# Output gates by tanh per chunk, one decay buffer refilled by halves, and a first chunk written out by hand

## The chip, the cores and the metric

The kernel runs on 1 core of one Trainium2 chip. The metric is device time in microseconds, from the start of the program to its end. Three timed runs of the kernel before gave 734.65 (median), 732.61 and 736.13; the execution that was profiled took 732.55, of which the profile's span is 730.6.

## The reference

Three stages follow each other. The first is a gated linear attention with a matrix state for every batch and head (4 batches, 8 heads, 768 tokens, 40 channels):

```python
m_new  = maximum(f_gate[t] + m, i_gate[t])
f_stab = exp(f_gate[t] + m - m_new);  i_stab = exp(i_gate[t] - m_new)
C = f_stab * C + i_stab * outer(v[t], k[t]);  n = f_stab * n + i_stab * k[t]
y[t] = sigmoid(o_gate[t]) * (C @ q[t]) / maximum(abs(n @ q[t]), 1)
```

The second is a mixture of 8 experts with one expert per token (320 to 1024 to 320), the third a gated layer of width 1536 with a sigmoid gate. Only the first stage is touched by the change.

## The kernel before, in words

The attention is computed in 24 chunks of 128 tokens (`NTILE`), 6 chunks (`NC`) to a batch. For a chunk, TensorE makes the matrix of log decays of all pairs of tokens (`dec`, L626), ScalarE takes its exponential (`exp`), TensorE makes the scores of q and k (`sc`), VectorE multiplies the two (`pf`), TensorE multiplies by v (`out_`, L665) on top of the part that comes from the state (`inter`), and POOL and TensorE build the update of the state (`kw`, `state`; then `Cm`, `C`, `cb`). Two groups of four heads each are worked on one after the other (`dec0`, `dec1`). After it come the denominator (`abs`, `den`), the output gate over the denominator (`sod`, POOL), the product (`x`), its split into two half-precision parts (`xh`, `xla`, `xl`), transposes and their evacuation by ScalarE (`tr`, `ev`), and the router's logits (`log`, `lg`).

All engines are scheduled by hand. `ORDER` (L40) lists the parts of one step with the lag in chunks: `sod:2` in step n works on chunk n-2. `step(n)` (L911) runs through that list once, and each engine executes in the order in which instructions are written. The entries `r:1` and `r:2` pull pieces from a generator, `step.route`: routing work of a group of chunks, or, in the first steps, the pieces of `rest()` (L597) and `second()` (L614).

The log decays come from gate sums. `gates(x)` (L481) makes them for all batches, one half (3 chunks of each batch) at a time, as a chain on VectorE with one piece on POOL and casts on ScalarE. `store(x)` writes them to DRAM, and `decay` (L411) reads them back into rows 0 to 15 of two operand tiles, `at` and `rt`, whose other rows hold a fixed pattern (`pattern_at`, `pattern_rt`). There are two pairs of these tiles: the first is for batches 0 and 2, the second for 1 and 3. The first pair is filled by halves, and from batch 1 on a whole batch is loaded in one go when the batch's first chunk is loaded. Chunk 0 does not wait for this way through DRAM: its `dec` (L628) adds up 16 small matmuls for each group of heads out of the gate rows themselves.

The raw output gates of a batch are one DMA of 960 KB on POOL's queue (`output_gates`, L448), written in steps 0 to 2 for batches 1 to 3. Batch 0's are turned into sigmoids by one ScalarE instruction in step 0 (L957), the other three batches' by three instructions at the start of step 5 (L923). Each time an exponential of a small tile is written behind (L958, L924). The loads of q, k (`load_qk`, three buffers) and v (`load_v`) are issued by SP in the order written; a load waits at its issue for the buffer to come free, and all later loads of SP wait behind it.

`begin()` (L551) writes the start: memsets by POOL, loads by SP and ScalarE, the first half of the gate chain, `store(0)`, `decay`. `warm(n)` (L590) writes n matmuls of zeros that keep TensorE active and whose result nobody reads: 26 in `begin`, and 4, 4, 8 and 6 in step 0. `to_end(x)` (L531) transposes the factors of a half to tokens on partitions: transposes, a VectorE copy, a small product on VectorE, a matmul, a copy.

Of the kernel before, what the change touches and what calls it, by code (L numbers as in the profile page):

```python
# [41 lines left out]
    Cm:0 r:1 log:3 scat:0 xh:2 r:1 out0:1 pf1:0 r:1 out1:1 lg:3 xla:2 inter:0 state:0 r:1 xl:2 abs:1 den:1  # L42
# [17 lines left out]
def fused(ctx, tc, a, out, dbg=None):  # L60
# [312 lines left out]
    with ExitStack() as att:  # L373
# [11 lines left out]
        ats = [a1.tile([KM, 2, 2, S], F16, name=f"at{i}") for i in range(2)]  # L385
        rts = [a1.tile([KM, 2, NC, NP, T], F16, name=f"rt{i}") for i in range(2)]
# [24 lines left out]
        def decay(b, c0=0, c1=NC):  # L411

            at, rt = ats[b % 2], rts[b % 2]
            tk = slice(c0 * T, c1 * T)
            src = a_d[:, :, 2 * b:2 * b + 2, tk].rearrange("n h g s -> (n h) g s")
            if c1 - c0 == NC:
                SP_.dma_start(out=at[0:8].rearrange("p i g s -> p i (g s)"),
                              in_=src.rearrange("p g s -> p (g s)").unsqueeze(1).to_broadcast([8, 2, 2 * S]))
            else:
                for i in range(2):  # L420
                    SP_.dma_start(out=at[0:8, i, :, tk], in_=src)
            for g in range(2):
                SP_.dma_start(out=rt[8:16, g, c0:c1].rearrange("p c h t -> p (c h t)"),
                              in_=L_d[:, 2 * b + g, :NP * LR].rearrange("n (h x) -> n h x", h=NP)[:, :, c0 * NP * T:c1 * NP * T])

        def load_qk(m):
            m.at, m.rt = ats[m.b % 2], rts[m.b % 2]
# [17 lines left out]
        def gate(b):  # L445
            return sos[b * NC // HT][:, b * NC % HT:][:, :NC]

        def output_gates(b, queue):  # L448

            queue.dma_start(out=gate(b).rearrange("p c h d -> p c (h d)"), in_=a["o"][b])  # L450
# [21 lines left out]
        def pattern_at(i, cs, copy):  # L472
            for k in range(2):
                copy(ats[i][:, k].rearrange("p g (c t) -> p g c t", t=T)[:, :, cs],
                     cat[:, k:k + 1, :].unsqueeze(1).to_broadcast([KM, 2, len(range(NC)[cs]), T]))

        def pattern_rt(i, cs):
            V.tensor_copy(rts[i][:, :, cs].rearrange("p g c h t -> p g c (h t)"),
                          crt.rearrange("p h t -> p (h t)").unsqueeze(1).unsqueeze(1).to_broadcast([KM, 2, len(range(NC)[cs]), NP * T]))
# [71 lines left out]
        def begin():  # L551

            G.memset(kws[1], 0.0)
            G.memset(blank, 0.0)
            A.activation(blank, blank, AF.Exp)
            warm(26)
            G.memset(qks[0], 0.0)
# [6 lines left out]
            SP_.dma_start(out=con[:, 0:2 + NP], in_=a["cc"])  # L564
            SP_.dma_start(out=own_row, in_=a["own_row"])
            load_qk(chunks[0])
            load_v(chunks[0])
            blocks_empty()
            SP_.dma_start(out=c32, in_=a["c32"])
            pattern_at(0, H0, lambda o, i: A.activation(o, i, AF.Copy))  # L570
            for t, name in ((c16, "c16"), (tok, "tok"), (wgl_s, "wgl"), (ctab, "ctab")):
                A.dma_start(out=t, in_=a[name])
# [7 lines left out]
            G.memset(Cbs[1], 0.0)  # L580
            pattern_rt(0, H0)
# [3 lines left out]
            decay(0, 0, HC)  # L585
            exps(0)
            load_qk(chunks[2])
            load_v(chunks[2])

# [7 lines left out]
        def rest():  # L597

            yield from gates(1)
# [8 lines left out]
            yield True  # L608
            yield True
            exps(1)  # L610
            decay(0, HC, NC)
            yield True

        def second():  # L614

            pattern_at(1, H0, V.tensor_copy)
            yield True
            pattern_rt(1, H0)
            yield True
            pattern_at(1, H1, V.tensor_copy)  # L620
            yield True
            pattern_rt(1, H1)
            yield True


        def dec(m, g):  # L626
# [12 lines left out]
            for i, rows in ((0, KM), (1, KM - 1)):  # L639
                cols = slice(64 * i, 64 * i + 64)  # L640
                PE.matmul(m.pw[g][:, :, cols], m.at[:rows, i, g, m.tk], m.rt[:rows, g, m.c, :, cols], start=True, stop=True)
# [83 lines left out]
        def sod(m):  # L725
            m.sod = ap_.tile([128, H, D], F32, name="sod")
            G.tensor_tensor(m.sod, sos[m.t // HT][:, m.t % HT], m.den.unsqueeze(2).to_broadcast([128, H, D]), ALU.mult)

        def x(m):
# [5 lines left out]
            V.scalar_tensor_tensor(m.x.rearrange("p (h d) -> p h d", d=D), m.po[:, :, 0:D], SX, m.sod, ALU.mult, ALU.mult)  # L735
# [111 lines left out]
        parts = dict(kw=kw, gs=gs, inter=inter, state=state, Cm=Cm, C=C, cb=cb, abs=abs_, den=den, sod=sod,  # L847
# [63 lines left out]
        def step(n):  # L911
# [3 lines left out]
            for i in LOADS.get(n, ()):  # L915
                load_weights(i)
            if 1 < n < NTILE - 2:
                load(chunks[n + 2])
            if n == 3:
                step.route = second()  # L920
            if n == 5:
                for b in range(1, B):
                    A.activation(gate(b), gate(b), AF.Sigmoid)  # L923
                A.activation(blank, blank, AF.Exp)  # L924
            for name, lag in order:
# [6 lines left out]
                elif name in ("tr", "ev", "log", "lg") and n >= NTILE or name == "kw" and n == 0:  # L932
                    pass
                elif 0 <= n - lag < NTILE:
# [9 lines left out]
                    if n == 0 and name == "exp0":  # L944
                        step.route = rest()
                    if n == 0 and name in ("sc0", "sc1"):
                        warm(4)
                    if n == 0 and name == "pf0":
                        to_end(0)
                        warm(8)  # L950
                        kw(chunks[0])
                    if n == 0 and name == "state":
                        warm(6)
# [61 lines left out]
        UPS = 6  # L1015
# [3 lines left out]
        with tc.manual_schedule(engines=manual):  # L1019
            begin()  # L1020
            step.drain = False
            for n in range(NTILE + 2):
# [397 lines left out]
```

## Time and profile before

| | |
|---|---|
| timed runs | 734.65 us median (732.61 to 736.13) |
| profiled execution | 732.55 us, span 730.6 us |
| TensorE busy | 704.7 us, 96% |
| VectorE, ScalarE, POOL busy | 400.6, 327.8, 116.9 us |
| mean granted TensorE clock | 0.981 |
| attention stage | about 0 to 152 us |
| ACT_TABLE_LOAD | 6, of 1.28 us each: L555, L957, L958, L923, L924, L1164 |

PE is TensorE's matmuls, PEld its weight loads, DVE VectorE, ACT ScalarE, SP the engine that issues most DMAs; a `q` behind the name (SPq, ACTq) is that engine's instruction queue with DMA issues and waits. A granted clock of 1.00 is 2.4 GHz and 0.50 is 1.2 GHz. Times of a timeline are counted from the span's start.

### The profile page before, as it was taken

How to read it: one execution, taken by the hardware profiler on the slowest of the kernel's cores; microseconds unless marked ns; L12 is line 12 of the kernel's file. 1: busy time of each engine (PE TensorE's matmuls, PEld its weight loads, DVE VectorE, ACT ScalarE, POOL GpSimd, SP SyncE). 2: the span in 40 equal slices, each digit the busy share in tenths (PEclk: the TensorE clock that was granted, in tenths of full speed). 3: DMA queues.
4: the chain of work that ended last, by engine and by line, in shares of the span. 5: the costliest groups of instructions: out<-in, count | busy, mean ns of one | idle time of the engine just before them, and what ended most of it. 6: DMA issues, size and time to landing. Idle time of an engine off the chain costs nothing. (4 is left out here: it accounts for less than half of the span.)

```text
span 730.6 us, 15424 instructions
## 1 busy us (share of the span) xinstructions
PE 704.7 (96%) x6069; PEld 495.0 (68%) x6069; DVE 400.6 (55%) x920; ACT 327.8 (45%) x763; POOL 116.9 (16%) x152
## 2 busy tenths in 40 slices
PE   8879999979989999999999999999999999999998
PEld 5668999967656675766755676666666666666665
DVE  5756878747778888888786830322303223132130
ACT  4687777726465666555554511322313223132231
POOL 4433466733111111111100000000000000000000
PEclk8998999999999999999999999999999999999999
DMA  6573455643999897984414203001020010000000
GB/s 192 182 222 105 145 183 182 216 136 103 267 272 274 259 288 224 261 231 140 133 57 109 55 19 89 3 9 46 1 55 1 10 46 1 28 1 10 19 1 27
DMA packets 66407, 84.02 MB, mean 115 GB/s; under 512 B 41253, under 2 KB 48630, under 8 KB 66334
## 3 DMA queue, kind: packets, MB, share of 16 engines
q1 hardware_dynamic: 62844, 70.62, 34.5%
q0 software_dynamic: 3056, 12.28, 4.7%
q8 instruction: 48, 0.79, 0.5%
q14 instruction: 25, 0.20, 0.1%
q10 hardware_dynamic: 434, 0.14, 0.1%
HBM read 57.53 MB, written 17.16 MB: 102 GB/s over the span
## 5 line engine op out<-in xcount | busy, mean ns | idle before, releaser
L125 PE MATMUL pa<-xT,wgv 128*128 128x384 f16 x1536 | 252.6, 327 | 2.1 <-DVE hh L1170 2.1
L125 PEld LDWEIGHTS <-wgv 128*128 128x128 f16 x1536 | 150.8, 98 | 102.4 <-issue 4.3
L1165 DVE SCALAR_TENSOR_TENSOR gt<-pa,sg 128x384 f32<-128x384 f32 x96 | 53.5, 557 | 225.0 <-PE pa L125 193.1
L1183 PE MATMUL pb<-wo,hh 128*128 128x320 f16 x864 | 118.5, 299 | 0.0
L1164 ACT ACTIVATE sg<-pa 128x384 f32<-128x384 f32 x96 | 47.0, 489 | 142.6 <-PE pa L125 142.5
L1183 PEld LDWEIGHTS <-hh 128*128 128x128 f16 x864 | 84.5, 98 | 33.2
L358 PE MATMUL pb<-w,hh 128*128 128x320 f16 (+4 forms) x624 | 87.3, 299 | 0.2
L125 PE MATMUL pa<-xT,w 128*128 128x384 f16 (+5 forms) x576 | 82.5, 304 | 2.6 <-DVE hh L348 2.6
L125 PEld LDWEIGHTS <-w 128*128 128x128 f16 x640 | 56.2, 99 | 34.3 <-issue 4.6
L358 PEld LDWEIGHTS <-hh 128*128 128x128 f16 (+4 forms) x624 | 62.7, 101 | 23.6 <-DVE hh L348 1.2
L112 DVE SCALAR_TENSOR_TENSOR w<-ws,w 128x512 f16<-128x512 f32 (+1 forms) x92 | 56.1, 639 | 6.2 <-ACT w L111 6.0
L111 ACT ACTIVATE w<-ws 128x512 f16<-128x512 f32 (+1 forms) x92 | 50.4, 592 | 15.0 <-DMA ws<-in_w 14.9
L1185 ACT ACTIVATE ob<-pb 128x320 f32<-128x320 f32 x24 | 10.5, 437 | 100.5 <-PE pb L1183 100.5
L650 PE MATMUL ps<-qk 128*128 128x128 f32 x384 | 51.9, 279 | 1.5 <-DMA qk<-in_qk 1.5
L1170 DVE TENSOR_TENSOR hh<-gt,hh 128x384 f16<-128x384 f32 x96 | 52.6, 548 | 0.7
L1169 ACT ACTIVATE hh<-gt 128x384 f16<-128x384 f32 x96 | 49.5, 516 | 6.0 <-DVE gt L1165 5.9
L650 PEld LDWEIGHTS ps<-qk 128*128 128x128 f32 x384 | 47.7, 195 | 2.7 <-issue 1.9
L369 POOL DMA_INDIRECT y_d<-yr,own x24 | 26.4, 1098 | 131.3 <-DVE w L112 40.0
L655 DVE TENSOR_TENSOR pf<-ps,w 128x512 f32<-128x512 f32 x48 | 32.9, 685 | 20.6 <-ACT w L645 18.0
L347 ACT ACTIVATE hh<-pa 128x384 f16<-128x384 f32 (+6 forms) x80 | 33.7, 432 | 14.9 <-PE pa L125 14.6
L348 DVE SCALAR_TENSOR_TENSOR hh<-pa,hh 128x384 f16<-128x384 f32 (+6 forms) x80 | 36.1, 477 | 5.0 <-ACT hh L347 4.8
L645 ACT ACTIVATE w<-pw 128x512 f32<-128x512 f32 x48 | 28.5, 593 | 6.6 <-PE pw L637 3.6
(192 smaller groups left out, 700.0 us busy)
## 6 DMA issues: line engine op xcount, KB each, us to landing
ws<-in_w SPq DMA_DIRECT2D x24, 512.0 KB
vk<-in_vk SPq DMA_DIRECT2D x24, 324.0 KB
qk<-in_qk SPq DMA_DIRECT2D x48, 160.0 KB
ws<-in_w SPq DMA_DIRECT2D x15, 480.0 KB
ws<-in_wg SPq DMA_DIRECT2D x9, 512.0 KB
ws<-in_wv SPq DMA_DIRECT2D x9, 512.0 KB
hh<-in_o POOLq DMA_DIRECT2D x4, 960.0 KB, 7.8
ws<-in_wo SPq DMA_DIRECT2D x8, 480.0 KB
```

The lines of the kernel that those rows point to most:

```text
L111: A.activation(hi, src, AF.Copy, scale=scale)
L112: low = lambda: V.scalar_tensor_tensor(lo, src, scale, hi, ALU.mult, ALU.subtract)
L125: PE.matmul(ps, r if swap else l, l if swap else r, start=n == 0, stop=n == len(steps) - 1)
L347: A.activation(self.hh[:, 0, f], ph, AF.Relu)
L348: V.scalar_tensor_tensor(self.hh[:, 1, f], ph, 0.0, self.hh[:, 0, f], ALU.max, ALU.subtract)
L358: PE.matmul(py, self.hh[:, x, k, sl], w2[:, y, k, :], start=k == 0 and x + y == 0, stop=k == K1 - 1 and x == 1)
L650: PE.matmul(m.ps[g][:, p, :], m.k2[:, g, p], m.q2[:, p], start=True, stop=True)
L1164: A.activation(sg, pgv[0], AF.Sigmoid, scale=1.0 / (SY * SWG))
L1165: V.scalar_tensor_tensor(gt, pgv[1], SGT / (SY * SWV), sg, ALU.mult, ALU.mult)
L1169: A.activation(self.gh[:, 0, f, :], box[0], AF.Copy)
L1170: V.tensor_sub(self.gh[:, 1, f, :], box[0], self.gh[:, 0, f, :])
L1183: PE.matmul(po, self.gh[:, x, k, sl], wo[:, y, k * DM:(k + 1) * DM], start=k == 0 and x + y == 0, stop=k == K2 - 1 and x == 1)
```

## The change

The sigmoid is written as (tanh(o/2) + 1)/2. Two new parts, `th` (ScalarE) and `th1` (POOL), do this in place for each chunk, one lag after the chunk; the factor 1/2 goes into the scale of `x`. The bulk Sigmoids of steps 0 and 5 are gone. The gates are loaded by half batches, the first two by POOL at the start and the other six by SP in every third step.

There is one pair `at`, `rt`. `decay(u)` refills one half of it (three chunks); it is written in every third step. `pattern_at` for both halves is made by ScalarE in `begin`, `pattern_rt` by VectorE, the second half in `rest`; `second()` is gone.

The start has another order: the pattern's source is loaded by ScalarE's queue, memsets move ahead of the gate chain or behind it (a copy of 8 elements of `L` by POOL holds back what follows it), one q/k buffer and the state's two operand tiles are zeroed by ScalarE. Step 0 is replaced by `first()`, which writes the parts of chunk 0 in their own order, its outputs included, with fewer filler matmuls and with two pieces of the second half of the gate chain ahead. The load of chunk 3 moves from the end of step 1 to `rest`, behind `decay(1)`.

```diff
 ORDER = """
-    Cm:0 ... inter:0 state:0 r:1 xl:2 abs:1 den:1
+    Cm:0 ... inter:0 state:0 r:1 xl:2 abs:1 th:1 den:1 th1:1
...
-        def decay(b, c0=0, c1=NC):
-            at, rt = ats[b % 2], rts[b % 2]
+        def decay(u):
+            b, c0 = u // 2, u % 2 * HC
+            c1 = c0 + HC
...
-            if m.first and m.b:
-                decay(m.b)
             load_qk(m)
             load_v(m)
...
+        def output_gates(u, queue):
+            c0 = u % 2 * HC
+            queue.dma_start(out=gate(u * HC, HC)..., in_=a["o"][u // 2][:, c0:c0 + HC])
...
         def begin():
+            copy = lambda o, i: A.activation(o, i, AF.Copy)
+            A.dma_start(out=con[:, 0:2 + NP], in_=a["cc"])
+            A.dma_start(out=own_row, in_=a["own_row"])
             G.memset(kws[1], 0.0)
             G.memset(blank, 0.0)
             A.activation(blank, blank, AF.Exp)
-            warm(26)
-            G.memset(qks[0], 0.0)
+            warm(WARM)
             V.memset(mm[:, 0:1], -1e30)
             G.memset(keep, 1.0)
             G.memset(c3(keep)[:, :, 0:1], 0.0)
-            G.memset(qks[1], 0.0)
+            G.memset(qks[0], 0.0)
+            G.memset(kws[0], 0.0)
...
+            copy(qks[1].rearrange("q x p t -> q x (p t)"), zeros.unsqueeze(1).to_broadcast([128, 3, NP * T]))
+            pattern_at(H0, copy)
+            pattern_at(H1, copy)
             for _ in gates(0):
                 pass
-            G.memset(kws[0], 0.0)
+            G.tensor_copy(blank, L[0:1, S // 2 - 8:S // 2])
             output_gates(0, G)
-            for t in (Cbs[0], qks[2]):
-                G.memset(t, 0.0)
+            G.memset(qks[2], 0.0)
+            output_gates(1, G)
+            pattern_rt(H0)
             factors(0, V)
...
+        def first():
+            m = chunks[0]
+            dec(m, 0)
+            dec(m, 1)
+            later = gates(1)
+            for _ in range(2):
+                next(later)
+            for g in range(2):
+                exp(m, g)
+                sc(m, g)
+                pf(m, g)
+            warm(2)
+            for t in Cbs:
+                A.activation(t.rearrange("q p j d -> q (p j d)"), kws[1]..., AF.Copy)
+            to_end(0)
+            kw(m)
+            for g in range(2):
+                out_(m, g)
+            state(m)
+            warm(3)
+            for t, name in ((c16, "c16"), (tok, "tok"), (wgl_s, "wgl"), (ctab, "ctab")):
+                A.dma_start(out=t, in_=a[name])
+            step.route = rest(later)
...
+        def rest(later):
+            yield from later
             yield
             store(1)
             yield True
             factors(1, G)
-            yield True
-            pattern_at(0, H1, V.tensor_copy)
-            yield True
-            pattern_rt(0, H1)
...
+            yield
+            pattern_rt(H1)
+            yield
             exps(1)
-            decay(0, HC, NC)
+            decay(1)
+            load(chunks[3])
             yield True
-
-        def second():
...
+        def th(m):
+            A.activation(gate(m.t)[:, 0], gate(m.t)[:, 0], AF.Tanh, scale=0.5)
+        def th1(m):
+            G.tensor_scalar_add(gate(m.t)[:, 0], gate(m.t)[:, 0], 1.0)
...
-            V.scalar_tensor_tensor(m.x..., m.po[:, :, 0:D], SX, m.sod, ALU.mult, ALU.mult)
+            V.scalar_tensor_tensor(m.x..., m.po[:, :, 0:D], SX / 2, m.sod, ALU.mult, ALU.mult)
...
         def step(n):
+            if n % HC == 0 and 0 < n < NTILE - HC:
+                decay(n // HC + 1)
+                output_gates(n // HC + 1, SP_)
             if 1 < n < NTILE - 2:
                 load(chunks[n + 2])
-            if n == 3:
-                step.route = second()
-            if n == 5:
-                for b in range(1, B):
-                    A.activation(gate(b), gate(b), AF.Sigmoid)
-                A.activation(blank, blank, AF.Exp)
...
-                    if n == 1 and name == "state":
-                        load(chunks[3])
-                    if n == 0 and name == "exp1":
-                        A.activation(gate(0), gate(0), AF.Sigmoid)
-                        A.activation(blank, blank, AF.Exp)
...
-                    if n < B - 1 and name == "state":
-                        output_gates(n + 1, G)
...
-        UPS = 6
+        UPS, WARM = 6, 22
...
             begin()
+            first()
-            for n in range(NTILE + 2):
+            for n in range(1, NTILE + 2):
                 step(n)
```

## Rows read from the trace of the kernel before

**Rows 1.** Waits of TensorE, 0 to 230 us: total, times, longest.
```profile
PE pl L125 <- ACT xTu L755: 7.9, 4, 5.4
```

**Rows 2.** Busy time of the engines in windows of single steps; PEclk is the granted clock.
```profile
core 0: us, PE busy (x) PEld busy (x) DVE busy (x) ACT busy (x) POOL busy (x), PEclk, DMA share, GB/s
...
48.50:60.12 11.62, 6.21 (x84) 5.78 (x82) 3.82 (x11) 10.08 (x14) 1.80 (x3) 0.73 0.26 72
60.12:64.76 4.64, 4.64 (x84) 4.46 (x83) 2.86 (x8) 2.51 (x6) 1.67 (x3) 0.93 0.59 167
85.12:89.57 4.45, 4.45 (x84) 4.28 (x82) 3.63 (x11) 3.06 (x8) 2.46 (x3) 1.00 0.63 185
89.57:93.90 4.33, 4.33 (x84) 4.21 (x82) 2.57 (x8) 2.51 (x6) 3.19 (x4) 1.00 0.56 172
25.23:30.62 5.39, 4.65 (x85) 4.27 (x84) 5.29 (x9) 4.56 (x13) 3.17 (x4) 1.00 0.42 164
30.62:36.93 6.31, 5.60 (x101) 5.25 (x98) 5.04 (x19) 3.53 (x11) 2.71 (x5) 1.00 0.83 244
36.93:43.58 6.65, 5.19 (x101) 4.82 (x98) 6.62 (x16) 4.07 (x12) 3.28 (x7) 1.00 0.94 321
```

**Rows 3.** Timeline of step 5: start, length, engine, line, operation.
```profile
47.67 1.28 ACT L923 ACT_TABLE_LOAD   x1
...
48.97 5.19 ACT L923 ACTIVATE hh<-hh 128x1920 f32<-128x1920 f32 x3
...
56.30 0.38 PE L125 MATMUL pl<-wgl,xTu 128*128 128x16 f16 x8 [5.41 <-ACT xTu L755]
```

**Rows 4.** TensorE alone in half-microsecond windows: busy, granted clock, DMA share, GB/s.
```profile
13.00:13.50 0.50, 0.50 (x3) 0.50 0.20 71
...
19.50:20.00 0.50, 0.50 (x4) 0.71 0.52 191
```

**Rows 5.** Timeline of VectorE and POOL in the first 25 us.
```profile
6.77 2.08 DVE L495 TENSOR_SCALAR w<-w 32x3 f32<-32x3 f32 x1
...
8.42 0.40 POOL L580 MEMSET Cb<- 128x328 f32 x1
...
24.51 0.15 DVE L495 TENSOR_SCALAR w<-w 32x3 f32<-32x3 f32 x1
```

**Rows 6.** Timeline of TensorE from the gate chain's end to chunk 0's outputs.
```profile
10.69 0.23 PE L636 MATMUL pw<-ws,w 8*128 8x128 f16 x1 [0.30 <-DVE w L504]
...
12.57 1.52 PE L595 MATMUL pz<-kw 128*128 128x512 f16 x4
...
18.13 1.85 PE L595 MATMUL pz<-kw 128*128 128x512 f16 x4
...
21.50 1.90 PE L595 MATMUL pz<-kw 128*128 128x512 f16 x8
...
23.93 1.47 PE L595 MATMUL pz<-kw 128*128 128x512 f16 x6
...
27.56 1.13 PE L673 MATMUL po<-vk,pf 128*64 128x41 f32 x32
```

**Rows 7.** Timeline of ScalarE, POOL and VectorE between steps 9 and 10.
```profile
83.70 0.45 ACT L739 ACTIVATE xsb<-x 128x320 f16<-128x320 f32 x1
...
84.12 0.16 ACT L719 ACTIVATE den<-po 128x8 f32<-128x8 f32 x1
...
84.23 0.71 POOL L742 TENSOR_TENSOR xsb<-x,xsb 128x256 f16<-128x256 f32 x1 [2.86 <-ACT lg L762]
...
85.32 0.70 ACT L755 ACTIVATE xTu<-pt 128x640 f16<-128x640 f16 x1 [1.03 <-PE pt L751]
...
85.35 0.72 POOL L727 TENSOR_TENSOR sod<-hh,den 128x320 f32<-128x320 f32 x1 [0.41 <-DVE den L723]
...
87.21 0.48 DVE L735 SCALAR_TENSOR_TENSOR x<-po,sod 128x320 f32<-128x320 f32 x1
```

**Rows 8.** Timeline: the loads of q and k for chunk 3, and their first reader.
```profile
32.17 1.32 SPq L431 DMA_DIRECT2D qk<-in_qk  x2
...
38.78 1.13 PE L650 MATMUL ps<-qk 128*128 128x128 f32 x8 [1.46 <-DMA qk<-in_qk]
```

More of the change, by code (lines that the diff above doesn't have):

```diff
@@ L41 @@
     r:1 gs:1 C:1 tr:3 dec0:0 sc0:0 ev:3 r:2 exp0:0 sod:2 cb:1 dec1:0 sc1:0 r:1 pf0:0 kw:0 r:1 x:2 exp1:0
-    Cm:0 r:1 log:3 scat:0 xh:2 r:1 out0:1 pf1:0 r:1 out1:1 lg:3 xla:2 inter:0 state:0 r:1 xl:2 abs:1 den:1
+    Cm:0 r:1 log:3 scat:0 xh:2 r:1 out0:1 pf1:0 r:1 out1:1 lg:3 xla:2 inter:0 state:0 r:1 xl:2 abs:1 th:1 den:1 th1:1
 """
@@ L384, in fused @@
         KM = 97
-        ats = [a1.tile([KM, 2, 2, S], F16, name=f"at{i}") for i in range(2)]
-        rts = [a1.tile([KM, 2, NC, NP, T], F16, name=f"rt{i}") for i in range(2)]
+        at = a1.tile([KM, 2, 2, S], F16, name="at")
+        rt = a1.tile([KM, 2, NC, NP, T], F16, name="rt")
         RING = 3
@@ L409, in fused @@
             chunks.append(m)
-        def decay(b, c0=0, c1=NC):
-            at, rt = ats[b % 2], rts[b % 2]
+        def decay(u):
+            b, c0 = u // 2, u % 2 * HC
+            c1 = c0 + HC
             tk = slice(c0 * T, c1 * T)
             src = a_d[:, :, 2 * b:2 * b + 2, tk].rearrange("n h g s -> (n h) g s")
[L416 to L421, printed above, removed]
+            for i in range(2):
+                SP_.dma_start(out=at[0:8, i, :, tk], in_=src)
             for g in range(2):
@@ L439, in load, with gate @@
         def load(m):
-            if m.first and m.b:
-                decay(m.b)
             load_qk(m)
             load_v(m)
[L445 to L450, printed above, removed]
+        def gate(t, n=1):
+            return sos[t // HT][:, t % HT:t % HT + n]
+        def output_gates(u, queue):
+            c0 = u % 2 * HC
+            queue.dma_start(out=gate(u * HC, HC).rearrange("p c h d -> p c (h d)"), in_=a["o"][u // 2][:, c0:c0 + HC])
         a3 = att.enter_context(tc.tile_pool(name="att3", bufs=2))
@@ L584, in begin @@
             load_v(chunks[1])
-            decay(0, 0, HC)
+            decay(0)
             exps(0)
@@ L588, in begin @@
             load_v(chunks[2])
+        def first():
[11 more added lines that the diff above has]
+            for t in Cbs:
+                A.activation(t.rearrange("q p j d -> q (p j d)"), kws[1].rearrange("p h x -> p (h x)")[:, :NP * 2 * DV], AF.Copy)
+            to_end(0)
[7 more added lines that the diff above has]
+            step.route = rest(later)
         def warm(n):
@@ L595, in warm @@
                 PE.matmul(pz, z[:, 0:128], z[:, 0:512], start=True, stop=True)
-        def rest():
-            yield from gates(1)
+        def rest(later):
+            yield from later
             yield
@@ L640, in dec @@
                 cols = slice(64 * i, 64 * i + 64)
-                PE.matmul(m.pw[g][:, :, cols], m.at[:rows, i, g, m.tk], m.rt[:rows, g, m.c, :, cols], start=True, stop=True)
+                PE.matmul(m.pw[g][:, :, cols], at[:rows, i, g, m.tk], rt[:rows, g, m.c, :, cols], start=True, stop=True)
         def exp(m, g):
@@ L726, in sod @@
             m.sod = ap_.tile([128, H, D], F32, name="sod")
-            G.tensor_tensor(m.sod, sos[m.t // HT][:, m.t % HT], m.den.unsqueeze(2).to_broadcast([128, H, D]), ALU.mult)
+            G.tensor_tensor(m.sod, gate(m.t)[:, 0], m.den.unsqueeze(2).to_broadcast([128, H, D]), ALU.mult)
+        def th(m):
+            A.activation(gate(m.t)[:, 0], gate(m.t)[:, 0], AF.Tanh, scale=0.5)
+        def th1(m):
+            G.tensor_scalar_add(gate(m.t)[:, 0], gate(m.t)[:, 0], 1.0)
         def x(m):
@@ L734, in x @@
             m.x = ap_.tile([128, DM], F32, name="x")
-            V.scalar_tensor_tensor(m.x.rearrange("p (h d) -> p h d", d=D), m.po[:, :, 0:D], SX, m.sod, ALU.mult, ALU.mult)
+            V.scalar_tensor_tensor(m.x.rearrange("p (h d) -> p h d", d=D), m.po[:, :, 0:D], SX / 2, m.sod, ALU.mult, ALU.mult)
         def xh(m):
@@ L845, in routing @@
                     break
-        parts = dict(kw=kw, gs=gs, inter=inter, state=state, Cm=Cm, C=C, cb=cb, abs=abs_, den=den, sod=sod,
+        parts = dict(th=th, th1=th1, kw=kw, gs=gs, inter=inter, state=state, Cm=Cm, C=C, cb=cb, abs=abs_, den=den, sod=sod,
                      x=x, xh=xh, xla=xla, xl=xl, tr=tr, ev=ev, log=log, lg=lg_)
@@ L931, in step @@
                         out_of(1)
-                elif name in ("tr", "ev", "log", "lg") and n >= NTILE or name == "kw" and n == 0:
+                elif name in ("tr", "ev", "log", "lg") and n >= NTILE or name[:3] == "out" and n == 1:
                     pass
```

40 lines of the change are left out of this document (6 added, 34 removed).

## The prediction

> **What bounds the kernel now.** I read the page's busy shares first, then TensorE's waits, then the busy time in windows cut at the first matmul of each chunk's decay (L641, or its direct form), then the timeline of the windows that stand out. The shares say TensorE, 96% of the span. So a change is worth something only where TensorE stands still or runs at its low clock, and it touches none of the expert stages: everything after 150 us should only move as a block. TensorE's longest wait of the attention stage is one of 5.4 us for the activation that evacuates the transposed rows [rows 1].
>
> The windows show the step sizes [rows 2]. Step 5, from 48.50 to 60.12, takes 11.62 us at a mean granted clock of 0.73, and step 6 takes 4.64 at 0.93. Steps of the same kinds later (last chunk of a batch, then first chunk of the next) take 4.45 and 4.33, with TensorE busy throughout. The timeline tells why [rows 3]: ScalarE loads the Sigmoid table for 1.28 us, runs three Sigmoids of 128x1920 for 5.19 us, loads the Exp table back, and only then evacuates the transposes; the logits' matmuls start at 56.30 after 5.41 us of waiting. Steps 1 to 3 take 5.39, 6.31 and 6.65 us [rows 2]. Before step 1 TensorE needs until 25.23 us for a first chunk whose own matmuls are few; most of that is filler, and from 13 to 19.8 us it ran at the lower of its two levels, 1.2 GHz [rows 4].
>
> **The change, part by part.** The sum is against the profiled execution's own time, 732.55 us (span 730.6 and about 2 around it); the median of the three timed runs, 734.65, lies 2.1 above it.
>
> *The Sigmoid block of step 5 goes.* With it go the wait and the slow clock behind it: (11.62 + 4.64) - (4.45 + 4.33) = 7.5 us [rows 2]. What is late next there? Nothing that I see: step 4 ran at full TensorE occupancy with the same other work, and step 10 is the same step without the block. Bounds: 7.5 if all goes, 6.5 if some of the tanh work below shows.
>
> *Tanh per chunk (`th`) on ScalarE.* No row has a tanh; the nearest is the 128x320 cast `xh`, 0.45 us [rows 7]. 24 of them are 10.9 us of ScalarE. They stand right behind `abs`, and there ScalarE is idle: `abs` ends at 84.28, and the evacuation `ev` begins at 85.32 after 1.03 us of waiting for TensorE's transposes [rows 7], which themselves wait for POOL's `xla`. A tanh of 0.45 ends by about 84.7, so it costs nothing; if it took more than 1.03 us, the excess would come back in every step, because ScalarE's and POOL's loop through `xh`, `xla`, the transposes and `ev` has little to spare against a step of 4.92. I take 0; bounds 0 and 0.2 a step.
>
> *`th1` on POOL.* A one-input add of 128x320: between a memset of 128x328 at 0.40 [rows 5] and the two-input product `sod` at 0.72 [rows 7]; I take 0.5. It stands between `xla` (ends 84.94) and `sod` (starts 85.35, when VectorE has the reciprocals), so it fills a gap of 0.4; `sod` moves by 0.1 to 0.35 us. Its reader `x` starts at 87.21, 1.1 us after `sod` ended [rows 7]. Queued behind it is `kw`, which the state's matmuls read much later in the step. Cost 0; bounds 0 to 0.1 a step, since steps with routing work have less slack on VectorE.
>
> The rows also show VectorE and POOL in each other's way: the 32x3 clamp of L495 takes 0.15 us alone and 2.08 us beside POOL's memsets, and it ends when they end [rows 5]. The Trainium skill (GPSIMD Engine Reference, Specifications) names contention of the two engines over SBUF where VectorE runs in a two-port mode or reads two SBUF inputs. By that rule `th1` speaks against the change, since it could hold VectorE's `den` for its own length; by the row's price of 0.5 us it would still end inside the 1.1 us above.
>
> *The startup.* The POOL memsets that held the clamp now come before or behind the gate chain, so the scan ends about 1.0 us earlier, and the subtraction before it about 0.3 earlier, as POOL's share starts sooner. The gate chain's end, where TensorE resumes at 10.69 [rows 6], moves to about 9.4; 22 instead of 26 filler matmuls ahead still cover it. From there TensorE's own order counts. In the kernel before, 22 filler matmuls stand between the two: 1.52 + 1.85 + 1.90 + 1.47 = 6.7 us [rows 6]. Five remain. Now the order at full clock: 9.4, rest of the first decay 0.9, second decay 1.3, eight plus eight score matmuls 2.1, two fillers 0.4, transposes to the end, wait for VectorE and side product 1.7, the two output halves 1.1 [rows 6], state 0.7, three fillers 0.6: 18.2 us for the first matmul of chunk 1, against 25.23. At the lower clock for as long as before (6.8 us, which costs 3.4) it is 21.6 [rows 4]. The clock fell after TensorE had waited in pieces behind the fillers, for the casts of the gates; these waits stay, which speaks for 21.6, and the shorter unbroken wait speaks for 18.2. I take the middle, 19.9: a gain of 5.3, bounds 3.6 and 7.0. The loads of chunk 1 and its decay rows are issued about 3 us earlier than before and land before that.
>
> *Constants by ScalarE's queue, zeroing and patterns by ScalarE.* The zeroing of a 128x1536 tile (1.4 us, as POOL's memset) and four pattern copies of 0.84 end at about 7.8 us, when the first gate cast is ready; 0 to 0.2 us, inside the middle above. The four late constant loads delay ScalarE by some 2.4 us after its last work of chunk 0, while TensorE is busy with the outputs and the state: 0. The Sigmoid and two table loads of step 0 ended before TensorE needed ScalarE again: 0.
>
> *Steps 1 to 3.* Chunk 0's outputs (1.13 us) leave step 1: 4.3. The second half of the gate chain now stands behind chunk 0's state copy on VectorE, so its end, the stores and `to_end(1)` in step 2 come later against the step. An estimate: from the state's end to the side product's factor VectorE has 16 operations, 8.5 us by their durations in the same steps before, and waits about 1.5 us in all for ScalarE's exponentials; TensorE's own work to that place is 8.1. So TensorE waits 1.9 us there, against 0.7 before: 1.2 more in step 2. In step 3 the scores waited 1.46 us for q and k of chunk 3 [rows 8], 5.3 us after their issue had ended, while four 960 KB gate loads shared the DMA engines; of these now two halves come in the startup and the next in step 3, which gives that wait back. Against it stands the queue: SP now issues the loads of chunk 4, then the half refill, then the loads of chunk 3, so the latter start about 4 us later against step 2. 5.39, 6.31 and 6.65 become about 4.3, 7.5 and 5.5 (4.92 and half a wait): a gain of 1.0; bounds a gain of 3.1 and a loss of 3.
>
> *One decay buffer.* From step 3 on a half is refilled every third step, three steps ahead. SP's issue waits for the decay matmuls of the step before, which are done, and behind it on SP stand only the gate load (one issue) and loads for two steps later: 0. The six copies of the pattern that VectorE no longer makes lay in steps where TensorE waited for DMA or nothing: 0.
>
> Sum: 7.5 + 5.3 + 1.0 = 13.8, that is 718.75 on the profiled execution's scale and 720.85 on the median's, 0.1 us from the 720.8 that I forecast.
>
> **The rivals.** *Tanh and Exp do not share a table.* The page shows a load of 1.28 us at each change between Exp and Sigmoid [rows 3], and none between Exp, Copy and Abs; of Tanh the trace says nothing. Two loads a step and the tanh are 3.0 us in a gap of 1.03: 2.0 us in each of 23 steps, 46 us, less 13.8: about 767. It decides for slower as soon as ScalarE's extra exceeds the gap by 0.6 us a step, so already one load with its tanh (1.74) does it. The Trainium skill (ScalarE: Activation LUTs, Table sets) lists tanh beside exp in one set. If that holds there is no load at all; I give this rival 0.05.
>
> *Only step 5 is won.* The half refill and the loads of chunk 3, queued on SP behind those of chunk 4, are late, and step 3 waits what the startup saved: 732.55 - 7.5 and up to 2.1 for the median, 725 to 727. For it: that wait exists already in a smaller form [rows 8]. Against it: less DMA traffic in those steps. 0.17.
>
> *Cold start.* With five fillers TensorE stays at the low level through steps 1 and 2; their 10 us of matmuls then cost 5 to 8 more: 726 to 729. For it: [rows 4] show it can last 6.8 us with TensorE busy. Against it: after step 5's wait, dense work from 56.30 brought the full clock back early in step 6 [rows 2, 3]. 0.08.
>
> **How the numbers follow.** The forecast, with its own range 716 to 724, has 0.67; only step 5, 0.17; cold start 0.08; table loads 0.05; 0.03 for losses that eat nearly all of it. A measurement here can tell about 0.5%, 3.7 us. Faster by more than that: the forecast and nearly all of the next two, 0.91; within it 0.03; slower 0.06. The range 715.5 to 727.5 takes in the first rival's time, the best startup (7.0 + 2 more) and part of the cold start.
>
> **What would show it.** After: no step of the windows above 8 us; four table loads fewer, and none between tanh and exp; the tanh at 0.45 us with `ev` still waiting for TensorE; the first L641 matmul at 18 to 22 us; the score matmuls of chunk 3 waiting under 2 us; from there on steps of 4.92. It is wrong if a table load stands beside each tanh, if steady steps are over 5.1 us, or if chunk 1 starts after 23 us.

## The result and the profile after

| | before | after |
|---|---|---|
| timed runs, side by side | 735.39 us median (732.61 to 738.05) | 726.67 us median (724.05 to 727.69) |
| ratio, 95% interval | | 0.9876 (0.983 to 0.9922) |
| profiled execution, its span | 732.55, 730.6 us | 726.39, 724.3 us |
| VectorE, ScalarE, POOL busy | 400.6, 327.8, 116.9 us | 396.7, 328.1, 144.8 us |

The change makes the kernel faster by 8.7 us, or 1.2%. The forecast was 720.8 us, a gain of 13.8. A second set gave 731.47 and 726.25 (ratio 0.9928, 0.99 to 0.9956), a gain of 5.2. Levels differ between chips (the kernel before took 735.82 us on one and 731.47 on another), so below the ratio within one set counts, and stages are compared in the traces. There the start of each chunk's first decay matmul is the milestone (L641 before, L651 after):

| stretch | before, us | after, us | gain | forecast |
|---|---|---|---|---|
| start to chunk 1 | 25.23 | 22.08 | 3.15 | 5.3 |
| steps 1 to 3 | 18.35 | 19.90 | -1.55 | 1.0 |
| step 4 | 4.92 | 4.93 | -0.01 | 0 |
| steps 5 and 6 | 16.26 | 8.79 | 7.47 | 7.5 |
| steps 7 to 22 | 79.12 | 82.47 | -3.35 | 0 |
| chunk 23 to the end | 586.72 | 586.13 | 0.59 | 0 |
| span | 730.6 | 724.3 | 6.30 | 13.8 |

One profile is one execution, and executions of one kernel differ: in the second set the changed kernel took from 723.44 to 731.65 us. The one profiled there, at 731.11, has nearly the same stages but for two. Steps 1 to 3 took 21.78 us, 1.88 more, and from chunk 23 to the end it took 589.01, 2.88 more. Step 3 alone was 1.86 longer, and chunk 4 started at 44.08 instead of 41.98:

```profile
36.37:44.08 7.71, 7.33 (x99) 6.62 (x98) 3.07 (x8) 4.29 (x13) 2.57 (x4) 0.65 0.52 163
```

So a difference of 2 us at chunk 4, or of 3 at the end, cannot be read from two single profiles. By step 7 the new kernel is 9.06 us ahead, and then it loses a third of that. In the windows by step (length, then busy time of PE, PEld, DVE, ACT and POOL, granted clock, DMA share, GB/s), the lines that answer to [rows 2] are these, steps 1 to 6 and then 7 to 22 as one:

```profile
22.08:26.72 4.64, 4.64 (x54) 4.28 (x52) 3.80 (x7) 3.79 (x12) 1.46 (x2) 0.74 0.42 123
26.72:36.13 9.41, 7.75 (x100) 7.34 (x98) 7.44 (x20) 5.00 (x15) 6.62 (x11) 0.74 0.56 158
36.13:41.98 5.85, 5.85 (x99) 5.67 (x98) 2.82 (x7) 4.29 (x13) 2.63 (x4) 0.83 0.71 211
41.98:46.91 4.93, 4.93 (x100) 4.78 (x98) 3.03 (x8) 4.18 (x13) 2.78 (x5) 1.00 0.49 137
46.91:51.37 4.46, 4.46 (x85) 4.29 (x83) 3.64 (x11) 3.42 (x9) 2.28 (x4) 1.00 0.57 159
51.37:55.70 4.33, 4.33 (x84) 4.21 (x82) 3.09 (x8) 2.87 (x7) 2.99 (x4) 1.00 0.82 229
55.70:138.17 82.47, 79.58 (x1510) 75.81 (x1508) 61.58 (x190) 64.09 (x194) 64.25 (x78) 1.00 0.67 202
```

The same stretch of the kernel before:

```profile
64.76:143.88 79.12, 78.08 (x1511) 75.17 (x1508) 61.46 (x188) 57.77 (x178) 47.51 (x61) 1.00 0.59 181
```

Steps 5 and 6 are now 4.46 and 4.33, to 0.01 us what the prediction set for them. In the last pair POOL's busy time stands out: 47.5 us became 64.3. Of TensorE's waits in the first 230 us, against [rows 1], these matter (total, times, longest):

```profile
PE pl L125 <- ACT xTu L771: 4.9, 3, 3.0
...
PE pl L540 <- DVE own_g L537: 2.4, 2, 1.7
PE pw L646 <- ACT w L496: 1.7, 1, 1.7
...
PE pt L767 <- POOL xsb L758: 1.1, 2, 0.6
```

The wait of 5.4 us is gone. New are one of 1.7 for a cast of the first gate chain (L496), one of 1.7 for the side product (L537), and transposes that wait for POOL (L758). The 3.0 for the evacuation stands in the last routing steps, after chunk 23, behind an idle ScalarE whose releaser the trace can't name.

ScalarE at the end of step 10, the same place as in [rows 7] (start, length, operation, idle time before it), has the tanh at 0.46 us between `abs` and `ev`, and `ev` still waits for TensorE:

```profile
75.35 0.16 ACT L729 ACTIVATE den<-po 128x8 f32<-128x8 f32 x1
75.41 0.46 ACT L740 ACTIVATE hh<-hh 128x320 f32<-128x320 f32 x1
76.55 0.70 ACT L771 ACTIVATE xTu<-pt 128x640 f16<-128x640 f16 x1 [0.68 <-PE pt L767]
```

Table loads fell from 6 to these two, none of them beside a tanh:

```profile
L554 ACT ACT_TABLE_LOAD x1 | 1.3, 1283 | 1.9 <-issue 1.9
L1160 ACT ACT_TABLE_LOAD x1 | 1.3, 1283 | 0.0
```

POOL in steps 21 and 22 shows the loss. From 126.63 to 138 it is never idle for more than 0.2 us:

```profile
129.69 0.73 POOL L673 TENSOR_TENSOR kw<-vk,tm 128x320 f32<-128x320 f32 x1
130.59 1.03 POOL L850 DMA_INDIRECT xs_d<-xsb,dest  x1 [0.17 <-issue]
131.65 0.68 POOL L758 TENSOR_TENSOR xsb<-x,xsb 128x256 f16<-128x256 f32 x1
132.29 1.02 POOL L743 TENSOR_SCALAR hh<-hh 128x320 f32<-128x320 f32 x1
133.39 0.72 POOL L737 TENSOR_TENSOR sod<-hh,den 128x320 f32<-128x320 f32 x1
134.27 1.06 POOL L850 DMA_INDIRECT xs_d<-xsb,dest  x1 [0.16 <-issue]
135.36 0.73 POOL L673 TENSOR_TENSOR kw<-vk,tm 128x320 f32<-128x320 f32 x1
```

One round, from `kw` to `kw`, takes 5.67 us, and step 21 takes 5.54 and step 22 5.66, where the kernel before needed 4.92 and 4.95. There the same round had one gap, 0.41 us ahead of `sod`, besides pauses of 0.15 to 0.17 ahead of the scatters:

```profile
136.13 0.73 POOL L663 TENSOR_TENSOR kw<-vk,tm 128x320 f32<-128x320 f32 x1
...
139.16 0.72 POOL L727 TENSOR_TENSOR sod<-hh,den 128x320 f32<-128x320 f32 x1 [0.41 <-DVE den L723]
...
141.08 0.73 POOL L663 TENSOR_TENSOR kw<-vk,tm 128x320 f32<-128x320 f32 x1
```

In these steps POOL, not TensorE, sets the pace. Of the 3.35 us, 2.15 arise in steps 19 to 22, the rest in steps 9, 12 to 15 and 18. The add (L743) takes 1.01 us; the two scatters of routed rows (L850) stand in the same queue, and the prediction did not count them.

In the startup, the line that answers to [rows 5] is the clamp, 0.16 us where it took 2.08, so the memsets no longer hold it. The chain's last result reaches TensorE at 10.05, 0.64 us earlier than before. TensorE however runs out of fillers (22 of them end at 7.5) and then waits:

```profile
7.19 0.16 DVE L491 TENSOR_SCALAR w<-w 32x3 f32<-32x3 f32 x1
```

```profile
1.30 6.23 PE L618 MATMUL pz<-kw 128*128 128x512 f16 x22 [1.30 <-POOL blank L553]
...
9.47 0.23 PE L646 MATMUL pw<-ws,w 8*128 8x128 f16 x1 [1.72 <-ACT w L496]
...
10.05 0.23 PE L646 MATMUL pw<-ws,w 8*128 8x128 f16 x1 [0.30 <-DVE w L500]
```

In the kernel before, 26 fillers lasted until 9.5:

```profile
1.32 8.15 PE L595 MATMUL pz<-kw 128*128 128x512 f16 x26 [1.32 <-POOL blank L554]
```

TensorE alone in windows (length, busy time, granted clock, DMA share, GB/s; against [rows 4]):

```profile
7.50:9.50 2.00, 0.28 (x4) 1.00 0.53 161
9.50:11.00 1.50, 1.20 (x17) 0.93 0.58 103
11.00:17.50 6.50, 6.50 (x37) 0.50 0.84 244
17.50:21.00 3.50, 2.79 (x59) 0.98 0.31 67
21.00:24.50 3.50, 3.50 (x15) 0.51 0.64 188
24.50:31.00 6.50, 5.11 (x68) 1.00 0.37 98
31.00:38.00 7.00, 6.73 (x80) 0.52 0.68 195
```

Three times a stretch in which TensorE stood still in part (0.28 of 2.00, 2.79 of 3.50, 5.11 of 6.50 us busy) is followed by one at 1.2 GHz (0.50). Before there was one such stretch in the startup. That standing still brings the low clock is my reading and not shown: in the kernel before TensorE waited 1.46 us ahead of chunk 3's scores [rows 8] and the clock stayed at 1.00, and ahead of the first stretch stand, besides the wait, the 32 small matmuls of chunk 0's decay. The three together last 17 us, and half of that, 8.5 us, is what full clock would have saved if nothing else had held TensorE. The third starts at the side product's wait, and VectorE's pattern copy ahead of that takes 2.04 us:

```profile
26.67 2.04 DVE L474 COPY rt<-ws 97x3072 f16<-97x3072 f16 x1
```

```profile
31.27 0.62 PE L540 MATMUL pl<-own_g,c 32*128 32x48 f32 x2 [1.66 <-DVE own_g L537]
```

### The profile page after: what moved, and what is told of

Its sections match the earlier page's. It is cut to its first block, busy times and chain, and to the rows that moved or that the text cites. A ratio compares the mean times of both kernels' runs of the same rounds, so it can differ in the third digit from the quotient of the medians.

```text
span 724.3 us, 15451 instructions
## 1 busy us (share of the span) xinstructions
PE 698.8 (96%) x6048; PEld 495.2 (68%) x6048; DVE 396.7 (55%) x912; ACT 328.1 (45%) x782; POOL 144.8 (20%) x172
## 5 line engine op out<-in xcount | busy, mean ns | idle before, releaser
L125 PE MATMUL pa<-xT,w 128*128 128x384 f16 (+5 forms) x576 | 80.9, 301 | 1.6 <-DVE hh L348 1.6
L660 PE MATMUL ps<-qk 128*128 128x128 f32 x384 | 53.9, 287 | 0.0
L369 POOL DMA_INDIRECT y_d<-yr,own x24 | 28.0, 1167 | 125.0 <-ACT w L111 19.5
L660 PEld LDWEIGHTS ps<-qk 128*128 128x128 f32 x384 | 49.9, 203 | 1.0 <-issue 0.2
L347 ACT ACTIVATE hh<-pa 128x384 f16<-128x384 f32 (+6 forms) x80 | 33.4, 431 | 13.8 <-PE pa L125 13.1
```

The costliest lines, as they stand in the source:

```text
L125: PE.matmul(ps, r if swap else l, l if swap else r, start=n == 0, stop=n == len(steps) - 1)
L347: A.activation(self.hh[:, 0, f], ph, AF.Relu)
L660: PE.matmul(m.ps[g][:, p, :], m.k2[:, g, p], m.q2[:, p], start=True, stop=True)
```

## The experiments

My theory after this: the loss of steps 7 to 22 is the add on POOL, and the startup lost its gain to waits that brought the low clock. Rivals: the half refills and SP's queue cost the steps (it was a rival ahead of the result), or VectorE has no room. Times are medians, each against the kernel before in the same set.

**The tanh alone.** The kernel before with only these edits: `th` and `th1` in `ORDER`, the bulk Sigmoids out. The four gate loads of a batch each and both decay buffers stay.

```diff
-            if n == 5:
-                for b in range(1, B):
-                    A.activation(gate(b), gate(b), AF.Sigmoid)
-                A.activation(blank, blank, AF.Exp)
```

> The kernel before with the tanh parts alone: th on ScalarE and th1 on POOL per chunk, factor 1/2 in x, the two bulk Sigmoid blocks gone; gate loads, decay buffers and the first chunk as before. The wait of 5.4 us in step 5 must go in any case (-7.5). Theory POOL: the add takes 1.0 us on POOL (measured in the changed kernel, where I had taken 0.5), and from step 9 on, where POOL also issues scatters, it lengthens the steps; steps 7 to 23 lose 3 us or more against the kernel before and the head of the first expert 1 to 2: 729 to 732 in all. Rival, the loss of the late steps comes from the half refills and gate loads on SP's queue: here no loss, steps 7 to 23 take 79.1 us as before, 726 to 728 in all.

731.7 us against 735.82, ratio 0.9937 (0.9911 to 0.9963): a gain of 4.1. In its profile steps 5 and 6 took 9.24 us, 7.02 less than before, and steps 7 to 22 took 82.71, 3.59 more:

```profile
59.46:142.17 82.71, 79.71 (x1510) 75.74 (x1508) 61.20 (x190) 64.22 (x194) 64.28 (x78) 1.00 0.59 174
```

There are no half refills in this kernel, so the loss comes with the tanh and the add; SP's queue is out. These two stages do not make up the whole: in the same profile chunk 1 started at 27.98, 2.75 later than before, with the low clock lasting from 12.5 to 26, and from chunk 23 on it took 588.43 us, 1.71 more. No run was made for that.

**The add on VectorE.**

```diff
-            G.tensor_scalar_add(gate(m.t)[:, 0], gate(m.t)[:, 0], 1.0)
+            V.tensor_scalar_add(gate(m.t)[:, 0], gate(m.t)[:, 0], 1.0)
```

> The changed kernel with the add of th1 on VectorE in place of POOL. Theory POOL: steps 7 to 23 (82.5 us in the changed kernel, 79.1 before) fall back to 79 to 80, POOL's busy time falls by 24 us, and the whole is 3 to 5 us shorter than the changed kernel: 721 to 724. Rival, SP's queue or the refills: steps 7 to 23 stay at 82.5 and the time at 726 to 727. A second rival, VectorE has no room either (it is 55% busy, about 75% in this stage): some steps with routing grow by the add's 0.3 us, and the gain is under 2 us.

726.71 us, ratio 0.9895 (0.985 to 0.994). The add takes 0.29 us, POOL is back at 47.7 busy, but steps 7 to 22 take 81.19: 1.3 of the 3.35 come back. TensorE's transposes now wait for VectorE's routing rows, 1.4 us in all. So the rival is half right: VectorE has no room in the routing steps either.

**A Sigmoid per chunk,** which prices the table loads of the prediction's first rival (no add, `x` scaled by SX):

```diff
-            A.activation(gate(m.t)[:, 0], gate(m.t)[:, 0], AF.Tanh, scale=0.5)
+            A.activation(gate(m.t)[:, 0], gate(m.t)[:, 0], AF.Sigmoid)
```

> The changed kernel with Sigmoid in place of the tanh in each chunk and no add: what the tanh would have cost had it not shared a table with Exp. The prediction's rival: two loads of 1.28 us and 0.45 us of work in a gap of 1.03 us, 2.0 us in each of 23 steps, so 724 + 46 less what POOL gets back without the add (3 to 5): 764 to 768. If part of the loads hides behind other waits, less: 745 to 760. No change at all would mean that no load is made.

763.57 us, one run. ScalarE in one step:

```profile
74.78 1.28 ACT L740 ACT_TABLE_LOAD   x1
76.08 0.47 ACT L740 ACTIVATE hh<-hh 128x320 f32<-128x320 f32 x1
76.57 1.28 ACT L795 ACT_TABLE_LOAD   x1
```

Two loads and the Sigmoid are 3.03 us, and steps 7 to 22 take 5.9 to 7.5. The price of that rival (about 767) was near: a step is 1.85 us longer than before on average, where 2.0 was taken. Its condition did not hold. The Trainium skill (ScalarE: Activation LUTs, Table sets) puts tanh into the set of exp and sigmoid into another; both traces agree, with no load beside 24 tanhs and, around 24 Sigmoids, 23 loads to them and 23 back.

**The second pattern copy early,** between chunk 0's two products, where TensorE has its own work:

```diff
                 pf(m, g)
+                if g == 0:
+                    pattern_rt(H1)
...
             yield
-            pattern_rt(H1)
             yield
```

> The changed kernel with the second pattern copy of rt (2.04 us on VectorE at the end of step 1) moved ahead, between chunk 0's two products, where VectorE waits for TensorE. Theory VectorE: the wait of 1.66 us for the side product of the second half in step 2 shrinks to 0.7 or less, TensorE keeps its full clock through steps 2 and 3 (it was at 1.2 GHz from 31.2 to 38.1 us), chunk 4's decay starts at 37.5 to 39 in place of 41.98, and the time falls by 3 to 4.5 us. Rival, the fillers that were cut hold the clock: the wait shrinks, but the clock falls all the same, and the gain is at most 1 us.

730.73 us, ratio 0.9912 (0.9887 to 0.9938): a miss. The wait for `own_g` fell only from 1.66 to 1.43, chunk 3 started 1.3 earlier, and then its scores waited for q and k, whose loads SP had issued at 31.75, and the clock fell again (chunk 4 at 43.70 instead of 41.98). This lies within what the startup does without the edit: in four profiles of it (the two of the changed kernel, the add on VectorE, and the add on ScalarE below) chunk 4 started at 40.30 to 44.08, and the scores of chunk 3 waited 0, 0.38, 1.07 and 1.94 us for q and k. In this run:

```profile
37.47 1.13 PE L661 MATMUL ps<-qk 128*128 128x128 f32 x8 [2.08 <-DMA qk<-in_qk]
```

**The add on ScalarE,** right behind the tanh:

```diff
-            G.tensor_scalar_add(gate(m.t)[:, 0], gate(m.t)[:, 0], 1.0)
+            A.activation(gate(m.t)[:, 0], gate(m.t)[:, 0], AF.Copy, bias=1.0)
```

> The changed kernel with the add of th1 done by ScalarE right behind the tanh (a Copy with bias 1), so that neither POOL nor VectorE has it. Before the evacuation of the transposes ScalarE still waited 0.68 us in a plain step with the tanh in it, and the add should take 0.46. Theory POOL (the loss of 3.35 us in steps 7 to 23 is the add's place on a full POOL): these steps take 79.1 to 79.8 us, the first expert's input arrives earlier too, and the whole is 3 to 5 us under the changed kernel: 722 to 724. Rival, the tanh itself and SP's new loads cost: 81 us or more stay, and the time is that of the changed kernel. A third outcome, ScalarE's gap is too small: each step grows by 0.1 to 0.3 us, 2 to 6 in all.

725.75 us against 730.32, ratio 0.9933 (0.991 to 0.9956). In steps 7 to 22:

```profile
57.48:137.30 79.82, 78.56 (x1510) 75.15 (x1508) 61.17 (x188) 71.00 (x211) 47.58 (x61) 1.00 0.71 208
```

That is 2.65 of 3.35 back, and steps 21 and 22 take 4.95 and 4.98: the theory of POOL holds. The whole shows nothing of it: the changed kernel on the same chip had 0.9928. In this profile step 3 waited 1.9 for q and k and chunk 4 started at 43.76, but the changed kernel profiled on that chip started it at 44.08, so this does not explain it. Why the whole gained nothing stays open.

**More fillers** ahead of the gate chain and between the transposes and the side product:

```diff
+            warm(4 if x == 0 else 6)
...
-        UPS, WARM = 6, 22
+        UPS, WARM = 6, 28
```

> The changed kernel with 28 in place of 22 filler matmuls ahead of the first chunk, and 4 and 6 fillers between the transposes of to_end and its side product, where TensorE waits 0.71 and 1.66 us for VectorE. Theory clock (the three stretches at 1.2 GHz, 10.8 to 17.6, 21.0 to 24.5 and 31.2 to 38.1, cost 8 us and follow TensorE's waits): at least the third goes, chunk 4's decay starts at 36 to 39 us in place of 41.98, and the whole is 3 to 6 us shorter. Rival, the clock falls because of the small matmuls and the waits for q and k, not for want of fillers: the low stretches stay, chunk 4 starts at 41 to 43, and the time is unchanged or 1 us longer.

725.71 us, ratio 0.9936 (0.9912 to 0.9959). The low stretches shrank to 13.0 to 16.2 and 36.5 to 40.4; chunk 3 started at 33.31, 2.8 earlier, but its scores waited 2.09 us for q and k again, and the second low stretch came behind that wait. Ahead of the first there was no wait left: TensorE was busy throughout from 7 to 13.0, from 9.8 to 12.4 with the small matmuls of chunk 0's decay. So the clock also falls without a wait that the profile shows, and the small matmuls, the rival of the expectation, are not excluded. Chunk 4 at 42.01: nothing kept.

**Chunk 3's loads earlier,** with the pattern copy early:

```diff
+            load(chunks[3])
             step.route = rest(later)
...
             decay(1)
-            load(chunks[3])
+            load(chunks[4])
```

> The changed kernel with the second pattern copy early (as in the fourth run) and another order on SP: the loads of chunk 3 at the end of the first chunk's part, the half refill ahead of the loads of chunk 4. Theory queue (with the pattern early, step 3 waited 2.08 us for q of chunk 3, issued only at 31.75 us behind chunk 4's loads and the refill, and the clock fell behind that wait): no wait of TensorE for q in step 3, one low stretch fewer, chunk 4's decay starts at 38 to 40 us against 43.70 there and 41.98 in the changed kernel; the whole 2 to 4 us under the changed kernel. Rival, DMA bandwidth and not the order decides: the wait moves to chunk 4 or to the refill and chunk 4 starts after 41.5.

724.74 us, ratio 0.992 (0.990 to 0.994). No wait for q and k; chunk 4 at 39.67, 2.3 earlier than in the changed kernel's first profile and 0.6 earlier than in any with the unedited startup. So the wait in the two misses goes with SP's queue; how much of the time goes with it one profile does not show. None of the last three edits (0.9933, 0.9936, 0.992) can be told from the changed kernel on this chip (0.9928) by its whole time.

**The add as a sum of two tensors,** on POOL as in the change, the second operand a broadcast of ones:

```diff
-            G.tensor_scalar_add(gate(m.t)[:, 0], gate(m.t)[:, 0], 1.0)
+            G.tensor_tensor(gate(m.t)[:, 0], gate(m.t)[:, 0], one1.unsqueeze(2).to_broadcast([128, H, D]), ALU.add)
```

> The changed kernel with the add on POOL written with two tensors (the second a broadcast of ones) in place of a tensor and a constant. If POOL's 1.01 us is the price of the constant form, the two-tensor form takes 0.72, as sod does on the same shape, and steps 7 to 23 fall from 82.5 to about 81; if it is the price of any add of this shape in place, it stays at 1.0.

724.35 us, one run. In steps 7 to 22, which took 81.86, the groups of POOL's two products by shape, total and mean ns:

```profile
L739 POOL TENSOR_TENSOR sod<-hh,den 128x320 f32<-128x320 f32 x16 | 11.6, 722 | 2.6 <-DVE den L735 0.8 <-DVE d L796 0.8
L745 POOL TENSOR_TENSOR hh<-hh,one 128x320 f32<-128x320 f32 x16 | 11.5, 719 | 2.3 <-ACT hh L742 2.3
```

0.72 instead of 1.01 us an add, and 0.6 us back.

**All three together:** fillers (WARM 30), pattern and loads early, the add on ScalarE; beside it the changed kernel again and a version with the add left on POOL.

> The changed kernel as it is, on the same chip as the two below: 0.988 to 0.994 of the kernel before, with low clock stretches around 11 to 17, 21 to 25 and 31 to 38 us, d4 (chunk 4's first decay product) at 42 or later, d7 to d23 about 82.2 us.

> The changed kernel with three edits together: more filler products ahead of and within the gate chain, the second pattern copy between chunk 0's two products with chunk 3's loads issued at the end of chunk 0's first part and the refill ahead of chunk 4's loads, and the add done by ScalarE. If the three losses are separate and add: no wait for qk, d4 at 36 to 39 us, d7 to d23 79.1 to 80.2 us, and the whole 5 to 8 us under the changed kernel. Rival (another wait takes over: the decay's landing, own_g, or the clock): d4 at 40 or later, or d7 to d23 above 81, and at most 2 us under the changed kernel.

> As the one above, with the add left on POOL. If the losses add: d4 as in that one, d7 to d23 82.2 us, and the whole some 2.5 us above it.

Against 731.47 before: changed again 726.25; with the add on POOL 723.79, ratio 0.988 (0.9833 to 0.9927), an interval that still overlaps the changed kernel's; all three 719.85, ratio 0.9839 (0.9803 to 0.9876). In the stages the losses add: with all three chunk 4 started at 38.56 and steps 7 to 22 took 79.80; with the add on POOL 38.08 and 82.24. The version with all three beats both kernels: 6.4 us under the changed one and 11.6 under the one before, though none of its edits showed in the whole time alone. That its span, 716.8, is 13.8 under that of before, the sum that I forecast, is luck: 2.2 of it lie behind chunk 23, where the two profiles of the changed kernel differ by 2.9. TensorE in the same windows:

```profile
7.50:9.50 2.00, 2.00 (x11) 1.00 0.54 165
...
11.00:17.50 6.50, 6.05 (x63) 1.00 0.81 246
17.50:21.00 3.50, 2.10 (x50) 1.00 0.17 46
21.00:24.50 3.50, 3.02 (x19) 0.74 0.60 171
```

With fillers up to the gate chain the full clock stays in this profile. In that of the version with the add on POOL, whose startup is written in the same way, it does not: without a wait TensorE ran at 1.2 GHz from 14.0 to 17.5.

```profile
11.00:17.50 6.50, 6.50 (x56) 0.74 0.82 245
```

So the first low stretch lasted 6.8 us with 22 fillers in the changed kernel, 3.2 with 28, and 3.4 or nothing with 30; what brings it is not shown. With all three edits chunk 1 still starts only at 21.21, because the decay rows are not there:

```profile
21.21 0.38 PE L654 MATMUL pw<-rt,at 97*128 97x256 f16 x2 [1.61 <-DMA rt<-L_d]
```

**The second gate load later.** In this version POOL issues the two gate loads of 480 KB at 8.81 and 10.86; the kernel before issued its one of 960 KB at 6.08. The DMA engines are 0.8 busy from 10 to 18, and SP issues the load of `rt` at 18.49, though the rows were stored 2.4 us earlier than before (there it issued it at 16.48).

```diff
-            output_gates(1, G)
             pattern_rt(H0)
...
             warm(3)
+            output_gates(1, G)
```

> The kernel with the three edits together (fillers, pattern and loads early, add on ScalarE), and in addition the second of the two 480 KB gate loads moved from the startup (issued at 10.86 us) to the end of chunk 0's part (about 21 us). If the gate loads are what holds chunk 1's decay rows back (DMA engines 0.8 busy from 10 to 18 us, SP issues the load of rt only at 18.5): rt issued by 17, no wait for rt, first decay product of chunk 1 at 19.6 to 20.2 instead of 21.2, and the whole about 1 us under the kernel with three edits (718.6 to 719.4 where that has 719.85). Rival (the way through DRAM takes this long by itself): rt issued within 0.3 us of 18.5, chunk 1 at 21 or later, same time.

Chunk 1's part came out as the theory had it: SP issued `rt` at 16.32, and chunk 1 started without a wait at 19.64; only its second group of heads waited:

```profile
13.66 1.33 SPq L419 DMA_DIRECT2D at<-a_d  x2
16.32 1.77 SPq L421 DMA_DIRECT2D rt<-L_d  x2
```

```profile
22.09 0.39 PE L654 MATMUL pw<-rt,at 97*128 97x256 f16 x2 [1.17 <-DMA rt<-L_d]
```

Chunk 4 started at 37.53, 1.0 earlier. The whole did not follow: 723.63 against 734.39, ratio 0.9853 (0.9828 to 0.9878), not to be told from the 0.9839. Chunk 23 started at 132.35, as without the edit, and the last routing steps had again a wait of 3.1 us for the evacuation.

## Why the prediction was right, and where it was not

Direction and range were right; the forecast was 5.9 us too fast. The range of 715.5 to 727.5 holds the time by 0.8 us; the forecast's own, 716 to 724, does not, so that the number came out right is owed to the width and in part to luck. Three of the prediction's own signs went against it: step 2 took over 8 us, chunk 1 started at 22.08 and not by 22, and steps 13, 14, 21 and 22, which took 5.03 or less before, took 5.16 to 5.66, where it had named steady steps over 5.1 as a sign of being wrong. Term by term:

- **The Sigmoid block, 7.5: measured 7.47.** What was taken from later steps of the same kind held.
- **Tanh, 0: right.** 0.46 us in a gap of 1.03, no table loads.
- **`th1`, 0: mis-sized.** 1.01 us where 0.5 was taken, above the upper bound of 0.72, which was a two-input product. The sentence that failed is that it fills a gap of 0.4 us between `xla` and `sod`: even without scatters it is 0.6 longer. And the gap was read in a step with one scatter, where POOL has others; in the last steps, with two, it is the only one, and POOL's queue becomes 5.67 us a round. Measured: 3.35 us over 16 steps, 0.21 a step where 0 to 0.1 was the bound; 2.65 of it goes when ScalarE does the add.
- **Startup, 5.3: measured 3.15**, under its bounds (3.6 to 7.0). Three steps failed. The gate chain's end was put at 9.4, 1.3 earlier, and came at 10.05: the clamp was shorter, but VectorE's first scan began at 3.78 instead of 3.30. "22 instead of 26 filler matmuls ahead still cover it": at the pace of the 26 before they would have ended at 8.2, they ended at 7.5, the matmuls behind the first casts started at 9.47, and the low clock followed from 11 to 17.5. And chunk 1's decay rows were to be issued 3 us earlier and land in time: SP issued the load of `rt` at 18.55, 2.1 later than before, and with all three edits the rows came at 21.2. So the full-clock end of the forecast, 18.2, was out of reach. That the gate loads, held back behind the scan, met the stores and the loads of chunk 1 is shown for the second of them: without it there `rt` was issued at 16.32 and chunk 1 started at 19.64. I had not asked what shares the DMA engines with these loads.
- **Steps 1 to 3, gain 1.0: measured a loss of 1.55**, inside the bounds; in the second profile 3.43, outside them. The wait in step 2 was forecast as 1.9 and measured as 1.66; what was not priced is the 1.2 GHz behind it. Step 2 took 9.41 instead of 7.5.
- **The queue rival** (chunk 3's loads behind chunk 4's, 0.17) has the measured time in its 725 to 727, but not by its mechanism: in the first profile the scores of chunk 3 did not wait. The wait was there in others, 0.38 to 1.94 us with the startup unedited and 2.1 where an edit brought chunk 3 forward, and it went when SP issued these loads earlier.
- **Cold start** (0.08): 726 to 729 was its time, and three low stretches are what it describes; but it named the five fillers in chunk 0. In the traces waits stand ahead of the stretches, and small matmuls ahead of the first; which of them brings the low clock no run separates.

Open stays the wait of 3 us in the last routing steps (ScalarE idle for 2 us; it is in the profiles of the changed kernel, of the first four experiments and of the last, and in none of the seven profiles taken on the chip of the second set, the changed kernel's among them). So it goes with the set rather than with an edit. No run was made for it.

## What to carry to other kernels

An engine that is "20% busy" is read in the step where its queue is fullest: add up the queue's round there, with its DMA issues, before hanging an operation on it. Where a change brings work forward, look at what its loads meet on the DMA engines and in the issuing queue. At startup count the fillers against the first real work: here too few left a wait, and a longer stretch of low clock went with it. And a stage of one profile is one execution: profile the same kernel twice before explaining 2 us.

## What the runs showed of the hardware

An add of a constant to 128x320 took 1.01 us on POOL, 0.47 on ScalarE and 0.29 on VectorE; a sum of two tensors of that shape took 0.72 on POOL. So with one input POOL was slower than with two. The Trainium skill (GPSIMD Engine Reference, Engine selection) has it the other way: two-input operations are about half as fast as on VectorE, one-input ones "roughly line-rate". No run here agrees with the second part, and the measurement decides. The pattern copy of 97x3072 on VectorE took 1.98 and 2.04 us in the changed kernel, beside a POOL memset of 1.40 and beside additions; between chunk 0's products, with POOL idle for most of it, 0.95 to 1.01. Beside the second copy the add on POOL took 1.77.
